# Shorter warm-up, earlier norms and reordered weight work in a one-core adaLN block (linear attention, then a dense Mish layer)

## The chip, the cores and the metric

The kernel runs on one core of one Trainium2 chip. The core has five engines that run side by side and wait for each other through semaphores: PE (TensorE, matrix products; its weight loads are listed as PEld), DVE (VectorE), ACT (ScalarE), POOL (GpSimd) and SP (SyncE, which here only asks for transfers). The metric is the device time of one execution in microseconds (us). All numbers are of the kernel as it was before the change.

## The reference

x has 2048 rows of 512 columns. A vector c gives six modulation rows. The first half is linear attention with 32 heads of 16 columns, the second a dense layer with Mish (512 to 1792 to 512):

```python
mod = (_silu(c) @ w_mod).reshape(c.shape[0], 6, 1, -1)
sa, ca, ga, sb, cb, gb = (mod[:, 0], mod[:, 1], mod[:, 2], mod[:, 3], mod[:, 4], mod[:, 5])
h = _layernorm(x, axis=-1) * (1 + ca) + sa
x = x + ga * _A_ref(h, A_wqkv, A_wo)
h = _layernorm(x, axis=-1) * (1 + cb) + sb
x = x + gb * _B_ref(h, B_w1, B_b1, B_w2)

# _A_ref, per head: phi(t) = where(t > 0, t + 1, exp(t)) + 1e-6
kv = phi(k)^T v;  z = sum of phi(k);  o = phi(q) kv / (phi(q) z + 1e-6);  out = o @ wo
# _B_ref
hid = x @ w1 + b1;  act = hid * tanh(softplus(hid));  out = act @ w2
```

## The kernel before

The 2048 rows are four blocks b of 512, and each block is four tiles t of 128 rows. A product in full precision is made of three in the fast 32-bit format: every operand is split into a high part (name ending in h, a cast on ACT or POOL) and a low part (ending in l, a subtraction on DVE), and PE adds high by high, high by low and low by high. So nearly every operand of PE passes through ACT or POOL and then DVE, and DVE has most of the work that isn't PE's.

The order on each engine is the order in which the program is written; nothing is rescheduled. Work that lies beside the main products is written as generators. `spawn` adds one to the running list, `spawn_idle` to a second list, and `tick` advances every running generator by one step and then the first two (later three) of the second list. So in one tick all that was spawned stands ahead of all that was spawned idle. All 128x512 tiles in SBUF come from one ring of 101 places (`SLOTS`); a load waits until the place it was given is free.

*Prologue (lines 111 to 620).* SP asks for x, the modulation weights and the first quarter of wqkv. Until the first data are there PE multiplies a tile of ones (`warm_up`, line 137): seven products, then the broadcast of silu(c) (`sc_bc`, line 148), then six (line 149). Block 0 is normalised tile by tile (`stats`, `act_sums`, `apply`), transposed on PE (`transposes_of`, line 498, with further warm-up products after the first two tiles), scaled by the modulation columns (`upper`, line 528, which needs mc from `mod_col`, line 179), and multiplied by wk into kp (lines 559 to 582). The first products of block 0 with x (`g_unit`, line 301, into gacc) need xn (the split of x) and pk (the split of phi(k)). `step(...)` advances single generators: `xsplit[t]` gives xn of tile t (its first step is the cast on POOL, its second the subtraction on DVE), `kpost[t]` gives phi(k) (ACT, then DVE's ku, then the cast pk_h on POOL and pk_l on DVE). Between these stands the normalisation of block 1: tiles 0 and 1 by `stats` on DVE, tiles 2 and 3 by `act_sums` on ACT; then `sums_eps` (DVE), the root on POOL (rs_x, line 205), `ln_shift` or `sums_shift` (DVE, nb_x), and `apply` on ACT. PE then transposes block 1 (line 243), and POOL and DVE split the result (hT), after POOL has made some constants (`make_constants`, line 158).

*First half of the dense layer (line 1197 on).* w1 and w2 are cut in seven pairs g of two times 128 hidden columns f. Each pair of hidden columns is computed for blocks 0 and 1 together with a seven-product scheme (`pair_unit`: p_a, p_s and the sums cb and c on DVE). PSUM has four tiles "acc", three "h" and one "tp", so a new p_s waits until DVE has read an older one (cb). The second product of block 0 (`d_unit`, into oacc) trails behind, by `trail`. For each f, `w2_job` (line 671) loads the 128 rows of w2, waits two ticks, multiplies them by gb on DVE (line 677), splits them and stores the halves to HBM. The first two are loaded ahead. SP's queue has, per pair, also the loads of w1 (w1p, `rows`), and the stores of w1's split parts (rd_, `store_rows`).

*Second product of block 1 (`second`, line 1182).* For f in the order 10 to 13, 0 to 9, PE multiplies a (block 1's hidden columns, split by `prep_a`) by w2, which is loaded back from HBM (w2b). Beside it `prepare` (line 1200) transposes the normalised blocks 2 and 3, `columns(2, c)` (line 954) makes the seven-product operands of these blocks from them (names b_2 and t_2, on ACT and DVE), and `w2_sums` makes sums of w2's rows. These operands are for the last part, blocks 2 and 3 together.

Of the kernel before, what the change touches and what calls it, by code (L numbers as in the profile page):

```python
# [18 lines left out]
NF = F // P  # L19
# [6 lines left out]
def block_kernel(ctx: ExitStack, tc: tile.TileContext, x, wqkv, wo, w1, b1t, w2, c, wmodt, out):  # L26
    nc = tc.nc
    act, dve, pool, pe, sp = nc.scalar, nc.vector, nc.gpsimd, nc.tensor, nc.sync
# [9 lines left out]
    def sb(name, dt=F32, shape=(P, 512)):  # L38

        return big.tile(list(shape), dt, tag="T", name=name, bufs=SLOTS)  # L40
# [9 lines left out]
    def spawn(gen):  # L50
        fresh.append(iter(gen))

    def spawn_idle(gen):

        idle_work.append(gen)
# [22 lines left out]
    def split(name, t, keep, key, lo_engine=dve, hi_engine=act, plus=None):  # L78

        hi, lo = sb(f"{name}h", F32R, t.shape), sb(f"{name}l", F32R, t.shape)  # L80
        if hi_engine is act:
            act.activation(hi, t, AF.Copy)
        else:
            hi_engine.tensor_copy(hi, t)
        if lo_engine is dve:
            yield
        if plus is None:
            lo_engine.tensor_tensor(lo, t, f32(hi), op=ALU.subtract)
        else:
            dve.scalar_tensor_tensor(lo, t, plus, f32(hi), op0=ALU.add, op1=ALU.subtract)  # L90
        keep[key] = hi, lo
# [45 lines left out]
    def warm_up(n):  # L137
        for i in range(n):
            pe.matmul(warm[:, P * (i % 4):P * (i % 4 + 1)], ones, ones, start=True, stop=True)
# [6 lines left out]
    dve.scalar_tensor_tensor(c2[0:1, :], th, 1.0, c0, op0=ALU.add, op1=ALU.mult)  # L146
    sc_bc = ps("acc", "sc_bc")
    pe.matmul(sc_bc, halves, c2, start=True, stop=True)
    warm_up(6)
    ident = cst.tile([P, P], F32, name="ident")  # L150
    make_identity(nc, ident)
    w32 = cst.tile([P, P], F32R, name="w32")
# [49 lines left out]
    def ln_rstd(key, b, lo=0, hi=4):  # L202

        y = rs[key, b][:, lo:hi]
        pool.tensor_tensor(y, y, half[:, lo:hi], op=ALU.pow)  # L205

    def ln_shift(key, b, lo=0, hi=4):

        dve.scalar_tensor_tensor(nb[key, b][:, lo:hi], mv[key, b][:, lo:hi, 0], -1.0, rs[key, b][:, lo:hi],  # L209
                                 op0=ALU.mult, op1=ALU.mult)  # L210

    def ln_apply(key, b, j, t, dst, engine):
        if engine is act:
            act.activation(dst, t, AF.Identity, bias=nb[key, b][:, j:j + 1], scale=rs[key, b][:, j:j + 1])  # L214
        else:
            engine.tensor_scalar(dst, t, mv[key, b][:, j, 0:1], rs[key, b][:, j:j + 1],
                                 op0=ALU.subtract, op1=ALU.mult)

    def act_sums(key, b, t, v):

        if (key, b) not in rs:
            for d, name in (rs, "rs"), (nb, "nb"):
                d[key, b] = cst.tile([P, 4], F32, tag=name, name=f"{name}_{key}_{b}", bufs=NB)
        scrap = sb(f"scrap_{key}_{b}_{t}")
        sums = cst.tile([P, 2], F32, tag="sums", name=f"sums_{key}_{b}_{t}", bufs=6)
        act.activation(scrap, v, AF.Identity, scale=-1.0 / D, accum_out=sums[:, 0:1])
        act.activation(scrap, v, AF.Square, bias=sums[:, 0:1], accum_out=sums[:, 1:2])
        return sums

    def sums_eps(key, b, t, sums):  # L230
        dve.tensor_scalar(rs[key, b][:, t:t + 1], sums[:, 1:2], 1.0 / D, EPS, op0=ALU.mult, op1=ALU.add)
        ln_rstd(key, b, t, t + 1)

    def sums_shift(key, b, t, sums):
        dve.tensor_tensor(nb[key, b][:, t:t + 1], sums[:, 0:1], rs[key, b][:, t:t + 1], op=ALU.mult)
# [31 lines left out]
    def k_post(p, b, t, hi_engine=act):  # L267
        u = ku[b, t] = sb(f"ku_{b}_{t}")
        yield from phi(p, f"k_{b}_{t}", u)
        yield from split(f"pk_{b}_{t}", u, pk, (b, t), hi_engine=hi_engine, plus=TINY)  # L270
        if b == NB - 1:
            dve.tensor_tensor(ku[0, t], ku[0, t], ku.pop((b, t)), op=ALU.add)
        elif b:
            pool.dma_start(ku[0, t], ku.pop((b, t)), accum_op=ALU.add)  # L274
# [189 lines left out]
    def stats(b, t):  # L464
        ln_stats("x", b, t, xt["x", b, t])
        ln_eps("x", b, t, t + 1)
        ln_rstd("x", b, t, t + 1)

    def apply(b, t, engine, shift=True):
        v = xt["x", b, t]  # L470
        if engine is act and shift:
            ln_shift("x", b, t, t + 1)
        ln_apply("x", b, t, v, v, engine)
# [24 lines left out]
    def transposes_of(*tiles):  # L498
        for t in tiles:
            for k in range(3):  # L500
                p = tp_late if k == 0 and t > 1 else tp0[k]
                pe.transpose(p[:, P * t:P * (t + 1)], xt["x", 0, t][:, P * k:P * (k + 1)], ident)
            warm_up(3 if t < 2 else 0)

    def mod_scale(k):
        mod_col(4 + k, sc_bc)
# [10 lines left out]
    xsplit = [split(f"xn_0_{t}", xt["x", 0, t], xn, (0, t), hi_engine=pool if t else act) for t in range(4)]  # L517

    def step(*gens):
        for g in gens:  # L520
            next(g, None)
# [49 lines left out]
    kpost = [k_post(kp[t], 0, t, pool) if t else k_post_first(kp[0]) for t in range(4)]  # L571
# [12 lines left out]
    step(xsplit[1], kpost[0], kpost[1])  # L584
    act.activation(sc_row, sc_bc, AF.Copy)
    stats(1, 0)
    step(kpost[0])
    sums2 = act_sums("x", 1, 2, xt["x", 1, 2])
    step(kpost[1], kpost[2])
    stats(1, 1)  # L590
    step(xsplit[1], kpost[1], kpost[3], xsplit[2])
    g_unit(0, 0)
    step(kpost[2])
    sums3 = act_sums("x", 1, 3, xt["x", 1, 3])
    sums_eps("x", 1, 2, sums2)
    ln_shift("x", 1, 0, 2)
    apply(1, 0, act, shift=False)
    apply(1, 1, act, shift=False)
    step(xsplit[2], kpost[2], xsplit[3])
    g_unit(0, 1)  # L600
    sums_eps("x", 1, 3, sums3)
    sums_shift("x", 1, 2, sums2)
    apply(1, 2, act, shift=False)
    step(kpost[3])
    sums_shift("x", 1, 3, sums3)
    apply(1, 3, act, shift=False)
# [60 lines left out]
    def load_w2(f):  # L667
        w2r[f] = sb(f"w2r_{f}")
        sp.dma_start(w2r[f], w2[P * f:P * (f + 1), :])

    def w2_job(f, wait=2):
        if f not in w2r:
            load_w2(f)
            for _ in range(wait):
                yield
        t = w2r[f]
        dve.tensor_tensor(t, t, bc["gb"], op=ALU.mult)
        yield
        yield from split(f"w2_{f}", t, w2s, f)
        yield  # L680
        g, n = f // 2, f % 2
        if n == 0:
            w2f[g] = drp.tile([P, 2, D], F32, name=f"w2f_{g}")
            for i in range(2):
                w2d[g, i] = drp.tile([P, 2, D], F32R, name=f"w2d_{g}_{i}")
        for i in range(2):
            pool.dma_start(w2d[g, i][:, n, :], w2s[f][i])
        if g < KEPT:
            pool.dma_start(w2f[g][:, n, :], t)
# [43 lines left out]
    def w2_again(f):  # L733

        w2s[f] = [sb(f"w2b_{f}_{i}", F32R) for i in range(2)]
        for i in range(2):
            pool.dma_start(w2s[f][i], w2d[f // 2, i][:, f % 2, :])  # L737
# [216 lines left out]
    def columns(c0, c, done):  # L954

        b11, b12, b21, b22 = [hf.pop((b, c + h)) for h in (0, 2) for b in (c0, c0 + 1)]
        t = [sb(f"t_{c0}_{c}_{i}") for i in range(4)]
        for d, u, v in (t[0], b12, b11), (t[1], b22, t[0]), (t[2], b22, b12), (t[3], b21, t[1]):
            dve.tensor_tensor(d, u, v, op=ALU.subtract)
        yield  # L960
        names = [("b11", b11), ("b21", b21), ("t1", t[0]), ("t2", t[1]), ("t3", t[2]), ("t4", t[3]), ("b22", b22)]
        halves = [split(f"{name}_{c0}_{c}", v, op_b, (name, c)) for name, v in names if name not in done]
        for n in range(0, len(halves) + 2, 2):
            for h in halves[max(n - 2, 0):n] + halves[n:n + 2]:
                next(h, None)
            yield
# [223 lines left out]
    def ahead(b, u):  # L1190

        if 0 <= u - NF + 4 < NF and last_first[u - NF + 4] < 2 * KEPT:
            w2_again(last_first[u - NF + 4])
        if 0 <= u - NF + 3 < NF:
            spawn(prep_a(b, last_first[u - NF + 3]))
# [4 lines left out]
    def prepare(f):  # L1200

        if f in (1, 3, 5, 7):
            for _ in range(2):
                transpose_f(*order.pop(0), "h")
        if f in (4, 8):
            spawn(columns(2, f // 4 - 1, ()))
        if f in W2_AT:
            spawn(w2_sums(W2_AT[f]))
        if f == NF - 2:
            load_rows(0)  # L1210
            load_wb(5)
        if f == NF - 1:
            load_wb(6)
# [15 lines left out]
    def trail(f, side=None, norm=True):  # L1229
        def unit():  # L1230
            if side is not None:
                if norm:
                    norm_next()
                spawn(side)
            d_unit(0, f, f)
            ahead(1, f)
        return unit

    for g in range(1, G):
# [217 lines left out]
```

## Time and profile before

| what | us |
|---|---|
| median of three runs | 494.65 |
| the three runs | 495.23, 494.62, 494.65 |
| the profiled execution, its own time | 495.11 |
| its span (first to last instruction) | 493.4 |
| DVE busy | 369.8 |
| ACT busy | 296.2 |
| POOL busy | 144.8 |

The span is what the trace shows; the execution's own time has some 1.7 us more around it. The granted clock of PE is 1.00 in every stretch of the trace. In a row of a timeline stand the start, the time, the engine, the line, the operation with the tiles that it writes and reads (buffer numbers left out, tile numbers kept where they follow an underscore), sizes, a count where equal rows follow each other, and in brackets how long the engine sat idle before it and what ended that. In a row of busy time by stretch stand the stretch, its length, the busy time of PE, PEld, DVE, ACT and POOL with the number of instructions, the granted clock, the share of the DMA engines' time and GB/s.

### The profile page before, as it was taken

The page shows a single profiled execution, that of the slowest core. Times are in us where ns is not written, and L with a number is a line of the kernel's source. Part 1 is how long each engine was busy: PE and PEld are TensorE (multiplying, and loading weights), DVE is VectorE, ACT ScalarE, POOL GpSimd, SP SyncE. Part 2 cuts the span into 40 slices and gives each one's busy share as a digit, 9 for nine tenths or more (in the row PEclk, how much of TensorE's full clock was granted, in tenths as well). Part 3 has the DMA queues.
Part 4 walks back from the last instruction along what each step waited for, and adds up shares of the span by engine and source line. Part 5 has one row for each costly group of instructions (what it writes and reads, how often), then busy time and mean ns, then how long its engine had stood idle before and what let it go on. Part 6 is the DMA issues. An engine that isn't in the chain of part 4 may idle for free.

```text
span 493.4 us, 7741 instructions
## 1 busy us (share of the span) xinstructions
PE 488.1 (99%) x2652; PEld 413.0 (84%) x2652; DVE 369.8 (75%) x717; ACT 296.2 (60%) x530; POOL 144.8 (29%) x244
## 2 busy tenths in 40 slices
PE   8999999999999999999999999999999999999997
PEld 7878888878878888888888878888888888899997
DVE  6888888999799698976877563789732666769872
ACT  6777587866546979738767655288045555568100
POOL 4493120000023123103432335214644410545200
PEclk9999999999999999999999999999999999999999
DMA  8714544144873417388899969999997704688512
GB/s 311 287 43 107 150 121 93 48 141 152 291 174 108 132 39 245 127 282 296 284 325 303 303 217 312 325 299 358 383 302 193 219 23 123 178 207 233 130 44 86
DMA packets 66785, 98.58 MB, mean 200 GB/s; under 512 B 7057, under 2 KB 31641, under 8 KB 66746
## 3 DMA queue, kind: packets, MB, share of 16 engines
q1 hardware_dynamic: 37896, 53.63, 32.9%
q0 software_dynamic: 28704, 44.19, 32.5%
q8 instruction: 21, 0.34, 0.3%
q10 hardware_dynamic: 146, 0.26, 0.1%
q14 instruction: 18, 0.15, 0.1%
HBM read 62.92 MB, written 33.03 MB: 194 GB/s over the span
## 4 chain that ended last, share of the span: by engine, by line
PE 97%; DVE 2%; POOL 1%; ACT 0%; issue 0%; ACTq 0%; POOLq 0%
PE p_a L1092 19%; PE p_s L1092 8%; PE oacc L76 5%; PE oacc L75 5%; PE oacc L74 5%; PE m L76 5%; PE m L75 5%; PE m L74 5%; PE o L74 3%; PE o L76 3%; PE o L75 3%; PE pq_a L371 3%; PE gacc L74 2%; PE gacc L76 2%; PE gacc L75 2%; PE pk L74 2%
## 5 line engine op out<-in xcount | busy, mean ns | idle before, releaser
L205 POOL TENSOR_TENSOR rs_n<-rs_n,half 128x1 f32<-128x1 f32 x16 | 11.4, 710 | 64.5 <-DVE rs_n L200 37.6
L1097 DVE TENSOR_TENSOR cb<-p_s,u 128x512 f32<-128x512 f32 x28 | 19.2, 686 | 12.8 <-ACT u L1133 12.8
L1127 ACT ACTIVATE u<-p_a 128x512 f32<-128x512 f32 x12 | 7.2, 598 | 28.3 <-PE p_a L1092 28.3
L1102 ACT ACTIVATE u<-p_a 128x512 f32<-128x512 f32 x14 | 8.4, 598 | 25.3 <-PE p_a L1092 25.3
L1084 ACT ACTIVATE ub<-cb,b1c 128x512 f32<-128x512 f32 x28 | 20.0, 718 | 5.8 <-DVE cb L1097 5.6
L1355 POOL DMA_DIRECT2D wt_m<-w2t x20 | 14.0, 702 | 26.8 <-DVE cb L1097 14.7
L949 ACT ACTIVATE hf_n<-tp_n,mc 128x512 f32<-128x512 f32 x16 | 11.7, 768 | 12.8 <-PE tp_n L947 12.8
L1133 ACT ACTIVATE u<-p_a 128x512 f32<-128x512 f32 x14 | 8.4, 596 | 17.0 <-PE p_a L1092 16.0
L737 POOL DMA_DIRECT2D w2b<-w2d x20 | 10.6, 534 | 24.0 <-PE tp_n L947 5.0
L1097 DVE TENSOR_TENSOR c<-p_a,u 128x512 f32<-128x512 f32 x14 | 9.6, 688 | 7.6 <-PE p_a L1092 6.5
L265 DVE SCALAR_TENSOR_TENSOR ku<-e_k,relu_k 128x512 f32<-128x512 f32 x15 | 10.7, 715 | 5.6 <-ACT relu_k L263 5.4
L849 POOL DMA_DIRECT2D rden_d<-rden x2 | 1.4, 718 | 45.7 <-DVE rden L847 45.7
L731 POOL DMA_DIRECT2D wb<-w2d x14 | 9.9, 710 | 14.7 <-PE p_a L1092 12.4
L1061 ACT ACTIVATE u<-p_a,b1c 128x512 f32<-128x512 f32 x14 | 9.6, 686 | 6.6 <-PE p_a L1092 6.6
L262 ACT ACTIVATE e_k<-pk 128x512 f32<-128x512 f32 x15 | 8.8, 589 | 7.8 <-PE pk L76 7.8
L214 ACT ACTIVATE x<-x,nb_x,rs_x 128x512 f32<-128x512 f32 x13 | 10.1, 810 | 5.4 <-DVE nb_x L209 3.8
L205 POOL TENSOR_TENSOR rs_x<-rs_x,half 128x1 f32<-128x1 f32 (+1 forms) x10 | 7.3, 736 | 20.4 <-DVE rs_x L200 19.6
L265 DVE SCALAR_TENSOR_TENSOR q<-e_q,relu_q 128x512 f32<-128x512 f32 x16 | 10.7, 684 | 3.1 <-ACT relu_q L263 3.1
L274 POOL DMA_DIRECT2D ku<-ku x8 | 7.2, 899 | 18.4 <-DVE ku L265 18.4
L873 DVE TENSOR_TENSOR r<-o,r 128x512 f32<-128x512 f32 x16 | 10.8, 676 | 1.0 <-PE o L76 0.9
L861 DVE SCALAR_TENSOR_TENSOR q<-q,rd 128x512 f32<-128x512 f32 x16 | 10.4, 683 | 1.4 <-DMA rd<-rden_d 1.4
L784 POOL DMA_DIRECT2D a1b<-rd_a x10 | 5.4, 539 | 19.0 <-PE p_a L1092 8.4
(1620 smaller groups left out, 1973.3 us busy)
## 6 DMA issues: line engine op xcount, KB each, us to landing
wm<-in_wmodt_dram SPq DMA_DIRECT2D x24, 256.0 KB, 5.2
w2b<-w2d POOLq DMA_DIRECT2D x20, 256.0 KB, 6.2
wt_m<-w2t POOLq DMA_DIRECT2D x20, 256.0 KB, 4.2
r<-in_x_dram SPq DMA_DIRECT2D x16, 256.0 KB, 2.9
x<-in_x_dram SPq DMA_DIRECT2D x15, 256.0 KB, 4.8
w1p<-in_w_dram SPq DMA_DIRECT2D x14, 256.0 KB, 3.5
w2r<-in_w_dram SPq DMA_DIRECT2D x14, 256.0 KB, 7.2
wb<-w2d POOLq DMA_DIRECT2D x14, 256.0 KB, 5.0
```

Source lines behind the costliest of these rows:

```text
L74: pe.matmul(o, st[0], mv[0], start=start, stop=False)
L75: pe.matmul(o, st[0], mv[1], start=False, stop=False)
L76: pe.matmul(o, st[1], mv[0], start=False, stop=stop)
L205: pool.tensor_tensor(y, y, half[:, lo:hi], op=ALU.pow)
L265: dve.scalar_tensor_tensor(dst, e, 1.0, r, op0=ALU.min, op1=ALU.add)
L371: pe.matmul(p, l, r, start=onto is None and c == 0 and i == 0, stop=c == 1 and i == 2, skip_group_check=onto is not None)
L873: dve.tensor_tensor(r, p, r, op=ALU.add)
L949: act.activation(hf[b, j], p, AF.Identity, bias=mc[:, 12 + j:13 + j], scale=mc[:, 16 + j:17 + j])
L1084: act.activation(u, p, AF.Mish, bias=b1c[:, f:f + 1])
L1092: pe.matmul(p, st, mv, start=onto is None and c == 0 and i == 0, stop=c == 1 and i == 2, skip_group_check=onto is not None)
L1097: dve.tensor_tensor(out, p, u, op=ALU.add)
L1355: pool.dma_start(v, w2t[g][:, :, SUM[name], :])
```

## The change

There are four edits.

1. `warm_up` after sc_bc makes four products instead of six; after the transposes of tiles 0 and 1 it makes two and one instead of three and three.
2. In the first block's tail, the steps are reordered. On POOL the cast xn_2h stands ahead of pk_1h instead of behind it, and the root for block 1's tile 3 stands ahead of xn_3h instead of behind it. On DVE `sums_eps` of tile 2 stands ahead of xn_1l instead of behind ku of tile 2, `sums_shift` of tile 2 directly behind `ln_shift`, and `sums_eps` of tile 3 ahead of pk_2l. Block 1's tiles 0, 1 and 2 are normalised on ACT in one go, behind the sums of tile 3 as before.
3. `load_w2` for f = 10 and 11 is called behind `d_unit` of f = 6, that of 12 and 13 behind f = 8. `w2_job` finds them loaded, and still waits its two ticks. On SP's queue the loads of 10 and 11 now stand directly behind those of 8 and 9, ahead of the loads of w1's last pair and the eight stores of pair 4; those of 12 and 13 stand behind these stores.
4. `columns(2, c)` is spawned idle. On DVE and ACT each a_4 to a_9 stands ahead of the operands of the last blocks that it stood behind, by up to two operations.

No operation is added on any engine; five products on PE are gone.

```diff
-    warm_up(6)
+    warm_up(4)
...
-            warm_up(3 if t < 2 else 0)
+            warm_up((2, 1, 0, 0)[t])
...
     stats(1, 0)
-    step(kpost[0])
+    step(xsplit[2], kpost[0])
     sums2 = act_sums("x", 1, 2, xt["x", 1, 2])
     step(kpost[1], kpost[2])
     stats(1, 1)
-    step(xsplit[1], kpost[1], kpost[3], xsplit[2])
+    sums_eps("x", 1, 2, sums2)
+    step(xsplit[1], kpost[1], kpost[3])
     g_unit(0, 0)
     step(kpost[2])
+    ln_shift("x", 1, 0, 2)
+    sums_shift("x", 1, 2, sums2)
     sums3 = act_sums("x", 1, 3, xt["x", 1, 3])
-    sums_eps("x", 1, 2, sums2)
-    ln_shift("x", 1, 0, 2)
-    apply(1, 0, act, shift=False)
-    apply(1, 1, act, shift=False)
-    step(xsplit[2], kpost[2], xsplit[3])
+    for t in range(3):
+        apply(1, t, act, shift=False)
+    step(xsplit[2])
+    sums_eps("x", 1, 3, sums3)
+    step(kpost[2], xsplit[3])
     g_unit(0, 1)
-    sums_eps("x", 1, 3, sums3)
-    sums_shift("x", 1, 2, sums2)
-    apply(1, 2, act, shift=False)
     step(kpost[3])
...
     def w2_job(f, wait=2):
         if f not in w2r:
             load_w2(f)
+        if f > 1:
             for _ in range(wait):
                 yield
...
         if f in (4, 8):
-            spawn(columns(2, f // 4 - 1, ()))
+            spawn_idle(columns(2, f // 4 - 1, ()))
...
             d_unit(0, f, f)
             ahead(1, f)
+            if f > 5 and f % 2 == 0:
+                for i in (4, 5):
+                    if f + i < NF:
+                        load_w2(f + i)
```

## The prediction

> **What bounds the kernel now.** I read the page first, then the waits of PE (TensorE), then the timelines of PE and its feeders where PE stood still.
>
> ```profile
> span 493.4 us, 7741 instructions
> PE 488.1 (99%) x2652; PEld 413.0 (84%) x2652; DVE 369.8 (75%) x717; ACT 296.2 (60%) x530; POOL 144.8 (29%) x244
> ...
> PE tp_x L243 <- ACT x L214: 0.4, 1, 0.4
> PE gacc L308 <- POOL pk_2h L84: 0.3, 1, 0.3
> PE p_s L1092 <- DVE cb L1097: 0.2, 1, 0.2
> ```
>
> PE is busy 99% of the span, and after its first instruction it has three waits of 0.2 to 0.4 us. Only two things can therefore bring time: fewer PE instructions on the path, or those few holes. A matmul's printed time overlaps with the next one's, so a hole's cost is read from starts: 128x512 products that follow each other start 0.227 us apart (four from 26.96 would end their turn at 27.87 in the rows below).
>
> **1. Fewer warm-up products.**
>
> ```profile
> 1.09 3.36 PE L139 MATMUL warm<-ones 128*128 128x128 f32 x14 [1.09 <-POOL ones L131]
> ...
> 6.37 1.76 PE L139 MATMUL warm<-ones 128*128 128x128 f32 x12
> 8.30 0.83 PE L139 MATMUL warm<-ones 128*128 128x128 f32 x6
> 10.28 0.30 PE L502 MATMUL tp_late<-ident,x 128*128 128x128 f32 x1
> 10.88 0.70 PE L563 MATMUL pk<-wk_0h,hT_x_0h 128*128 128x512 f32 x2
> ...
> 6.67 2.65 ACT L214 ACTIVATE x<-x,nb_x,rs_x 128x512 f32<-128x512 f32 x3
> 10.95 0.56 ACT L530 ACTIVATE hT_x_0h<-tp_late,mc 128x256 fp32r<-128x256 f32 x1 [1.10 <-PE tp_late L502]
> 12.30 0.79 ACT L530 ACTIVATE hT_x_1h<-tp_x,mc 128x512 fp32r<-128x512 f32 x1
> ...
> 10.78 0.68 DVE L181 SCALAR_TENSOR_TENSOR wm<-wm,sc_bc 128x512 f32<-128x512 f32 x1
> ```
>
> After sc_bc the calls of warm_up ask for 6+3+3 products, and now for 4+2+1: five fewer, ten instructions in the trace, where each product is two (6 show as x12). Six take from 8.30 to about 8.97, 0.112 us each, so at most 1.12 us goes. The path has a floor: the transposes of tile 2 need ACT's third normalisation, which ends at 6.67+2.65 = 9.32. PE would be there at 10.28-1.12 = 9.16, waits, and starts tp_late at about 9.37 where it started at 10.28: 0.91 earlier. ACT sat idle 1.10 us for just this transpose, so it follows. The next floor is hT_x_1h: its modulation column comes from DVE at 10.78+0.68 = 11.46, and no part of the change moves that, so ACT's 12.30 can become 11.5 and not less. I take 0.80 us, with bounds 0 (a later floor I overlook) and 1.12. What is late next is DVE's chain of columns and low halves, which also follows ACT's rows; the loads it reads were asked for earlier and do not move.
>
> **2. Second block's norms earlier.**
>
> ```profile
> 26.96 1.07 PE L308 MATMUL gacc<-pk_1l,xn_1h 128*128 128x512 f32 x4
> 28.36 1.19 PE L308 MATMUL gacc<-pk_2h,xn_2h 128*128 128x512 f32 x4 [0.33 <-POOL pk_2h L84]
> 31.21 0.49 PE L243 MATMUL tp_x<-ident,x 128*128 128x128 f32 x3
> 32.06 1.64 PE L243 MATMUL tp_x<-ident,x 128*128 128x128 f32 x13 [0.36 <-ACT x L214]
> 34.47 1.08 PE L308 MATMUL gacc<-pk_3h,xn_3l 128*128 128x512 f32 x4
> ...
> 23.93 0.61 POOL L84 CAST pk_1h<-ku 128x512 fp32r<-128x512 f32 x1 [3.23 <-DVE ku L265]
> 25.84 0.70 POOL L84 CAST xn_2h<-x 128x512 fp32r<-128x512 f32 x1
> 27.16 1.14 POOL L84 CAST pk_2h<-ku 128x512 fp32r<-128x512 f32 x1 [0.61 <-DVE rs_x L231]
> 29.46 1.06 POOL L205 TENSOR_TENSOR rs_x<-rs_x,half 128x1 f32<-128x1 f32 x1
> 33.77 0.61 POOL L84 CAST hT_x_0h<-hf_x 128x512 fp32r<-128x512 f32 x1
> ...
> 25.99 1.10 DVE L265 SCALAR_TENSOR_TENSOR ku<-e_k,relu_k 128x512 f32<-128x512 f32 x1
> 27.02 0.14 DVE L231 TENSOR_SCALAR rs_x<-sums_x 128x1 f32<-128x1 f32 x1
> 31.19 0.81 ACT L214 ACTIVATE x<-x,nb_x,rs_x 128x512 f32<-128x512 f32 x1 [0.83 <-DVE nb_x L235]
> ```
>
> The first hole: PE was due at 27.87 and began at 28.36, and those four took 0.12 more than the four before; 0.61 us in all. It waited for POOL's pk_2h, which waited for DVE's ku. That ku took 1.10 us where the DVE operation of that kind at 10.78 took 0.68, and xn_2h ran on POOL beside it. xn_2h now goes ahead of pk_1h, into POOL's 3.23 us of idleness, so ku should lose some 0.4 us. Against it stand one more tiny DVE operation ahead of ku (sums_eps, 0.14 at 27.02) and a second rs_x on POOL behind pk_1h (up to 1.06, the row at 29.46), which takes the place of xn_2h (0.70) and so still ends about when ku does. I take 0.35 us, bounds -0.14 and 0.61.
>
> The Trainium skill, page SBUF — State Buffer, section "SBUF: two separate sides", says that DVE and GpSimd share a port pair as an exclusive lock, held for the whole instruction, and that the loser blocks. The rows agree for ku (1.10) and pk_2h (1.14 against 0.61 for pk_1h). By it pk_2h itself may stay slow, since DVE's xn_2l still follows ku; the sum would lose nothing that it counts.
>
> The second hole: three transposes at 0.11 us from 31.21 end their turn at 31.54, and the fourth came at 32.06, with 0.05 more to get going: 0.57 us. It waited for the normalised tile 3, which ACT began at 31.19 because rs_x stood at 29.46 on POOL behind pk_2h and xn_3h. In the new order rs_x comes directly behind pk_2h and tile 2's bias is long done, so ACT can start tile 3 once POOL and DVE have done one small operation each: pk_2h's end, 28.30 less 0.35, plus 1.06 and 0.14 is 29.15, two us earlier. I take all 0.57, bounds 0 and 0.57. Late next is POOL's hT_x_0h at 33.77, behind pk_3h and the constants; pk_3h leaves that same rs_x behind it, so this row moves up by about 1 us, more than PE gains here.
>
> **3. w2's last rows.**
>
> ```profile
> 257.49 1.05 SPq L669 DMA_DIRECT2D w2r<-in_w_dram  x2
> 258.71 8.82 SPq L744 DMA_DIRECT2D w1p<-in_w_dram  x2
> 273.48 10.09 SPq L669 DMA_DIRECT2D w2r<-in_w_dram  x4
> DMA to landing us min/median/max: 3.6/5.8/7.8
> ...
> 281.07 0.69 DVE L677 TENSOR_TENSOR w2r<-w2r,gb_bc 128x512 f32<-128x512 f32 x1 [1.18 <-DMA w2r<-in_w_dram]
> 283.00 0.69 DVE L677 TENSOR_TENSOR w2r<-w2r,gb_bc 128x512 f32<-128x512 f32 x1 [1.24 <-DMA w2r<-in_w_dram]
> 289.11 0.68 DVE L1097 TENSOR_TENSOR cb<-p_s,u 128x512 f32<-128x512 f32 x1
> ...
> 289.26 0.39 PE L1092 MATMUL p_a<-b_3h,a_6l 128*128 128x512 f32 x1
> 289.85 0.50 PE L1092 MATMUL p_s<-t_0h,s_6h 128*128 128x512 f32 x1 [0.19 <-DVE cb L1097]
> ```
>
> DVE lost 1.18+1.24 = 2.42 us to w2's rows 10 and 11, then worked without a pause, and its cb ended 0.36 us too late (289.85-289.26-0.23), with 0.11 for the restart: 0.47 us. The loads of 10 and 11 now stand on SP behind those of 257.49, ahead of the two w1p and the eight stores; those of 12 and 13 behind the stores. One of the two waits for a ring place, as w1p did; even if both left as late as the second w1p (267.5) and took 7.8 us, they land at 275.3, before DVE wants them (279.9). Behind them on SP wait w1p of pair 6, which then leave by about 268, as before. The same bytes move, so I charge DMA with nothing. I take 0.47; bounds 0 and 0.47.
>
> **4. Last blocks' operands behind all else.**
>
> ```profile
> 346.61 0.68 DVE L88 TENSOR_TENSOR a_8l<-ub,a_8h 128x512 fp32r<-128x512 f32 x1
> 346.96 0.39 PE L75 MATMUL oacc<-w2b,a_8h 128*128 128x512 f32 x1
> 347.35 0.50 PE L76 MATMUL oacc<-w2b,a_8l 128*128 128x512 f32 x1
> 340.00:352.00 12.00, 12.00 (x53) 9.45 (x52) 11.96 (x20) 5.30 (x10) 8.26 (x15) 1.00 1.20 367
> ```
>
> DVE is full here (11.96 of 12 us), and a_8l came 0.16 us late, plus 0.11: 0.27 us. In the new order two operations that start 0.60 us apart no longer stand before a_8l, so it comes 1.2 us earlier. No instruction is added. The operands put behind are for products after 352 and all done in the same ticks. I take 0.27, bounds 0 and 0.27.
>
> **Sum.** 0.80+0.35+0.57+0.47+0.27 = 2.46 us. The profiled execution took 495.11 us, 1.7 more than its span, so it becomes 492.65. The median of before is 494.65, from 495.23, 494.62 and 494.65: two groups half a us apart. If that half is noise everywhere, the sum gives 492.2; if it lies in the first 10 us, where PE's early pace decides and the change leaves ACT as the floor, 492.65. I say 492.5.
>
> **The rivals.** (a) The prologue's gain stops short: part 1 gives 0 because a load or DVE becomes the floor. For it: DVE is the tight engine there. Against: ACT's 1.10 us of waiting was for PE. Time 492.5+0.8 = 493.3. (b) The two late parts bring nothing (0.74): the transfers are late in the new place too, or another DVE operation is as late. Against: 4.6 us of margin at 275.3. Time 493.2. (c) DVE cannot follow in the second block: PE arrives 2.2 us earlier (all but part 4), DVE's full stretch does not move, and a_8l (1.2 earlier) leaves PE standing 2.2-1.2+0.1 = 1.1 us. Time 492.5+0.27+1.1 = 493.9. Against: the stretch begins behind ACT's copies of PE's transposes, so it moves with PE. (d) The other side: PE loses its pace. In the first 3.4 us an instruction takes 0.24 us, later 0.112: PE starts at half pace. The warm-ups fill the time between transposes; with fewer of them PE is idle for some 0.4 us more, in short pieces, between 8.3 and 9.4. If PE falls to half pace near 10 us for a stretch of 7 us, it loses 3.5 us, and the time is 496.0. It decides for slower from a stretch of (495.64-492.5)x2 = 6.3 us on; the start, from 1.09 to 6.37 at least, shows that 5.3 are possible. Against: from 31.21 to 33.45 PE had only transposes and a hole of 0.52, and four products then took 1.08 us, as before.
>
> On (d), the Trainium skill's page TensorE: Matmul & The Clock Gate, section "Part 4: PE-mode transpose", says that transposes do not count as PE-busy in the same way, and its Part 1 that PE drops to half clock after an idle window of about 3.4 us. By that rule (d) is likelier than a count of instructions suggests; the row at 34.47 speaks against it, since the clock held there. (e) The change does not do what it says: each engine's order is moved as the words have it, but each hole reappears one step later, and only the 0.35 of xn_2h is kept: 494.3. Against: two of the four holes have DVE rows without a pause behind them, so a shift of DVE passes through.
>
> **How the numbers follow.** All main terms land: 0.62, and 492.5, with a range of its own of 491.9 to 493.2. (a) 0.12, (b) 0.09, (c) 0.05, (d) 0.06, (e) 0.06. What a measurement can tell from no change is about 0.2%, 1.0 us, so faster means under 493.66. Main, (a) and (b) lie there: 0.83, less 0.01 for their upper ends. (c) and (e) are within: 0.11, with 0.01 from (a). Slower is (d) and a rest: 0.07. The range goes from 491.6 (all upper bounds, 1.12+0.61+0.57+0.47+0.27 = 3.04, off 494.65) to 493.9.
>
> **What would show it.** Right: tp_late near 9.4, hT_x_1h near 11.5, the two holes near 28 and 31 gone or under 0.3 us, no DVE wait for w2r and PE's p_s directly behind p_a near 287, no hole at a_8l. Wrong: PE instructions of the first matmuls at twice their pitch (d), or a new wait of PE on DVE near 345 (c) or on POOL's hT rows near 34 (e).

## The result, and the profile after

| | before | changed |
|---|---|---|
| median of seven runs, us | 494.68 | 493.52 |
| lowest to highest | 494.52 to 495.59 | 493.07 to 494.08 |
| ratio, 95% interval | | 0.997 (0.9958 to 0.9981) |
| span of the profiled execution | 493.4 | 492.0 |

By the medians the change makes the kernel 1.2 us faster. The forecast was 492.5, in a range of 491.6 to 493.9.

PE does the same products in the same order in both kernels, but for five warm-up products. So the gain can be followed by one product at a time: its start before, its start after.

| PE's product | before | changed | earlier by |
|---|---|---|---|
| tp_late, first transpose of tile 2 | 10.28 | 9.38 | 0.90 |
| pk by hT_x_1h | 13.23 | 12.49 | 0.74 |
| pk by hT_x_1l | 16.08 | 15.47 | 0.61 |
| first gacc (pk_0h, xn_0h) | 22.42 | 22.38 | 0.04 |
| gacc by pk_2h | 28.36 | 28.24 | 0.12 |
| gacc by pk_3h and xn_3l | 34.47 | 33.78 | 0.69 |
| p_a by a_6l, last before the stop at 289 | 289.26 | 288.67 | 0.59 |
| p_s by s_6h, first behind it | 289.85 | 288.89 | 0.96 |
| oacc by a_8l | 347.35 | 346.01 | 1.34 |

The 0.90 us of the warm-ups were there at 10 us and were gone at 22. Of the second part the tile 3 half stayed (0.12 to 0.69), and the two late parts stayed too. The page and PE's waits of the changed kernel:

```profile
span 492.0 us, 7721 instructions
...
PE 487.3 (99%) x2642; PEld 411.7 (84%) x2642; DVE 370.8 (75%) x717; ACT 296.4 (60%) x530; POOL 146.1 (30%) x244
...
PE gacc L308 <- POOL pk_2h L84: 0.2, 1, 0.2
```

Of PE's three waits, those for tile 3's norm and for cb are gone; that for pk_2h is left.

**Where the first 0.9 us went.** The timelines of the changed kernel, PE's first, then DVE's low halves and POOL's work on wk:

```profile
12.49 1.17 PE L563 MATMUL pk<-wk_1h,hT_x_1h 128*128 128x512 f32 x4
14.42 1.08 PE L570 MATMUL pk<-wk_0h,hT_x_0l 128*128 128x512 f32 x4
15.47 1.20 PE L570 MATMUL pk<-wk_1h,hT_x_1l 128*128 128x512 f32 x4
...
19.48 0.74 PE L575 MATMUL pk<-wk_3h,hT_x_3l 128*128 128x512 f32 x2
...
22.38 1.12 PE L308 MATMUL gacc<-pk_0h,xn_0h 128*128 128x512 f32 x4
...
11.59 1.44 DVE L551 TENSOR_TENSOR hT_x_0l<-hf_x,hT_x_0h 128x512 fp32r<-128x512 f32 x1
14.34 1.08 DVE L551 TENSOR_TENSOR hT_x_1l<-hf_x,hT_x_1h 128x512 fp32r<-128x512 f32 x1
17.73 1.09 DVE L88 TENSOR_TENSOR xn_0l<-x,xn_0h 128x512 fp32r<-128x512 f32 x1
18.75 0.68 DVE L551 TENSOR_TENSOR hT_x_3l<-hf_x,hT_x_3h 128x512 fp32r<-128x512 f32 x1
...
10.48 0.62 POOL L84 CAST wk_1h<-wr 128x512 fp32r<-128x512 f32 x1 [1.42 <-DMA wr<-in_wqkv_dram]
11.18 1.30 POOL L88 TENSOR_TENSOR wk_1l<-wr,wk_1h 128x512 fp32r<-128x512 f32 x1
```

The same of the kernel before:

```profile
12.45 0.69 DVE L551 TENSOR_TENSOR hT_x_0l<-hf_x,hT_x_0h 128x512 fp32r<-128x512 f32 x1 [0.98 <-ACT hf_x L530]
...
14.46 0.94 DVE L551 TENSOR_TENSOR hT_x_1l<-hf_x,hT_x_1h 128x512 fp32r<-128x512 f32 x1
...
9.96 0.61 POOL L84 CAST wk_1h<-wr 128x512 fp32r<-128x512 f32 x1 [0.92 <-DMA wr<-in_wqkv_dram]
10.66 1.29 POOL L88 TENSOR_TENSOR wk_1l<-wr,wk_1h 128x512 fp32r<-128x512 f32 x1
```

DVE used to sit idle for 0.98 us before hT_x_0l. ACT now has its operand ready 0.86 us sooner, and DVE begins at 11.59 where it began at 12.45. But there it meets POOL's wk_1l, which runs to 12.48, and takes 1.44 us where it took 0.69. hT_x_1l starts 0.12 earlier than before, takes 1.08 for 0.94 beside POOL's wk_2l, and ends at 15.42, 0.02 later than before (15.40). Before, PE asked for it at 16.08; now PE is there at 15.34 (the four of 14.42 and 4 times 0.23), waits, and starts at 15.47. xn_0l (1.09 us) stands before hT_x_3l, which ends at 19.43, and PE, due at 19.35, starts at 19.48. Each stop also costs some 0.1 for the restart: the second product behind it comes 0.34 us after the first, where 0.23 is the rule. POOL, for its part, was 0.52 us later than before, because the load of wk_1 landed later. No part of the change touches that load, and the changed kernel's second profile (below) has the cast at 10.05.

**The second block.** ku has its normal length, pk_2h has not, and tile 3 is in time. The changed kernel's rows of POOL, DVE, ACT and PE, and then one of DVE in the kernel before:

```profile
21.02 0.61 POOL L84 CAST xn_2h<-x 128x512 fp32r<-128x512 f32 x1
27.04 1.15 POOL L84 CAST pk_2h<-ku 128x512 fp32r<-128x512 f32 x1 [0.26 <-DVE nb_x L209]
...
21.14 1.03 DVE L285 SCALAR_TENSOR_TENSOR pk_0h<-e_k,relu_k 128x512 fp32r<-128x512 f32 x1 [0.71 <-ACT relu_k L282]
26.29 0.68 DVE L265 SCALAR_TENSOR_TENSOR ku<-e_k,relu_k 128x512 f32<-128x512 f32 x1
...
27.04 0.68 DVE L88 TENSOR_TENSOR xn_2l<-x,xn_2h 128x512 fp32r<-128x512 f32 x1
...
30.10 0.82 ACT L214 ACTIVATE x<-x,nb_x,rs_x 128x512 f32<-128x512 f32 x1 [0.55 <-DVE nb_x L235]
...
28.24 1.20 PE L308 MATMUL gacc<-pk_2h,xn_2h 128*128 128x512 f32 x4 [0.19 <-POOL pk_2h L84]
...
31.10 1.91 PE L243 MATMUL tp_x<-ident,x 128*128 128x128 f32 x16
```

```profile
21.25 0.69 DVE L285 SCALAR_TENSOR_TENSOR pk_0h<-e_k,relu_k 128x512 fp32r<-128x512 f32 x1 [1.18 <-ACT relu_k L282]
```

In its new place POOL's xn_2h no longer runs beside ku, but it runs beside DVE's pk_0h, which starts 0.11 us earlier than before and takes 1.03 for 0.69. This, and sums_eps (0.07), which now stands before xn_1l, puts DVE's row back, and ku starts at 26.29 for 25.99. The four experiments below show that it is this part of the change that does it: pk_0h takes 1.04 in the one with the norms moved and 0.69 in the other three.

The 16 transposes run as one group from 31.10; before, they were three, a stop, and thirteen.

**The two late parts.** SP's, DVE's and PE's rows of the changed kernel:

```profile
256.80 6.20 SPq L669 DMA_DIRECT2D w2r<-in_w_dram  x4
...
279.22 1.29 DVE L678 TENSOR_TENSOR w2r<-w2r,gb_bc 128x512 f32<-128x512 f32 x2
...
288.67 0.39 PE L1093 MATMUL p_a<-b_3h,a_6l 128*128 128x512 f32 x1
288.89 0.39 PE L1093 MATMUL p_s<-t_0h,s_6h 128*128 128x512 f32 x1
...
344.45 0.68 DVE L88 TENSOR_TENSOR a_8l<-ub,a_8h 128x512 fp32r<-128x512 f32 x1
...
345.79 0.39 PE L75 MATMUL oacc<-w2b,a_8h 128*128 128x512 f32 x1
346.01 0.39 PE L76 MATMUL oacc<-w2b,a_8l 128*128 128x512 f32 x1
```

The loads of w2's rows 10 and 11 leave with those of 8 and 9, DVE takes both rows one behind the other with no wait, and PE's p_s follows p_a by 0.22 us. a_8l ends at 345.13, 0.9 us before PE wants it.

### The profile page after: what moved, and what is told of

Read it like the earlier page. It is cut to its first block, busy times and chain, and to the rows that moved or that the text cites. A ratio compares the mean times of both kernels' runs of the same rounds, so it can differ in the third digit from the quotient of the medians.

```text
span 492.0 us, 7721 instructions
## 1 busy us (share of the span) xinstructions
PE 487.3 (99%) x2642; PEld 411.7 (84%) x2642; DVE 370.8 (75%) x717; ACT 296.4 (60%) x530; POOL 146.1 (30%) x244
## 4 chain that ended last, share of the span: by engine, by line
PE 96%; DVE 2%; ACT 1%; POOL 0%; ACTq 0%; issue 0%
PE p_a L1093 19%; PE p_s L1093 8%; PE oacc L75 5%; PE oacc L76 5%; PE oacc L74 5%; PE m L76 5%; PE m L75 5%; PE m L74 5%; PE o L74 3%; PE o L76 3%; PE o L75 3%; PE pq_a L371 3%; PE gacc L74 2%; PE gacc L76 2%; PE pk L76 2%; PE gacc L75 2%
```

## The experiments

Theory F says: in the prologue DVE's row of columns and low halves is the floor, and PE cannot keep what the warm-ups gave. Theory L adds: the floor moves with the landing of wk_1's load, because POOL's wk_1l follows the load and DVE's hT_x_0l is held up by wk_1l. Rival N is the term of the prediction, 0.80 us kept.

**Each part alone, in the kernel before.** The first:

```diff
-    warm_up(6)
+    warm_up(4)
...
-            warm_up(3 if t < 2 else 0)
+            warm_up((2, 1, 0, 0)[t])
```

> The kernel before with the fewer warm-up products alone. Theory F (floor): DVE's row of modulation columns and low halves up to hT_x_3l sets when PE may go on, whatever else happens; PE is some 0.8 us early at 12 us and has given nearly all of it back by its first gacc product, which starts between 22.3 and 22.4 us (22.42 before); time 494.6, no more than 0.15 below before. Rival L (landing): the profile of the changed kernel had wk_1's load land 0.5 us later by chance (POOL's cast at 10.48, before 9.96), and POOL's later row slowed DVE; where the cast starts near 9.96, the first gacc product comes at 22.0 or earlier and the time is 494.0 to 494.3. Rival N (the prediction's term): 0.80 us kept, first gacc at 21.6, time 493.9.

Measured: 494.42, ratio 0.9988 (0.9977 to 0.9999); the first gacc at 22.28 with the cast of wk_1h at 10.44. Of the 0.78 us that PE had at tp_late (9.50 for 10.28) 0.14 were left, so in this execution N is out. The time alone does not show it: the median is 0.62 below that of the kernel before beside it (495.04), and the interval allows 0.05 to 1.1.

The second has the whole reordering of steps from the change:

```diff
-    step(kpost[0])
+    step(xsplit[2], kpost[0])
...
+    sums_eps("x", 1, 2, sums2)
+    step(xsplit[1], kpost[1], kpost[3])
...
+    for t in range(3):
+        apply(1, t, act, shift=False)
```

> The kernel before with the norms moved alone. The second hole (tile 3's transposes) goes: 0.5 to 0.57 us. For the first hole (pk_2h at 28 us) theory F says: DVE's ku is no longer slowed (0.68 for 1.10), but pk_2h's cast on POOL still takes about 1.1 since DVE's xn_2l runs beside it; with DVE's row not pushed back by the prologue the hole shrinks from 0.49 by 0.3 to 0.4: together 0.85 to 0.95, time 493.7 to 493.9. Rival: the first hole stays at 0.36 or so as in the changed kernel, whatever the prologue did, since the added bias and norm operations of DVE take back what ku gains: together 0.63, time 494.0.

Measured: 494.75, ratio 0.9996 (0.9984 to 1.0008): nothing. The trace shows why. The second hole is gone and the first has shrunk only a little, so that the transposes behind them come 0.67 us earlier than in the kernel before, and 0.12 of it PE had already at the first gacc (22.30). The 0.55 between is the rival's side, and what took ku's gain is pk_0h beside xn_2h, as above. And then at 285 and 289 us most of the gain is lost again, by DVE's and PE's rows of this kernel:

```profile
282.22 1.32 DVE L677 TENSOR_TENSOR w2r<-w2r,gb_bc 128x512 f32<-128x512 f32 x2 [3.09 <-DMA w2r<-in_w_dram]
...
289.68 0.50 PE L1092 MATMUL p_s<-t_0h,s_6h 128*128 128x512 f32 x1 [0.45 <-DVE cb L1097]
```

PE came earlier, the load of w2's rows did not: DVE waited 3.09 us for it instead of 2.42, and p_s started only 0.17 us before its time in the kernel before. Without the third part the second is worth little in such an execution.

The third:

```diff
             load_w2(f)
+        if f > 1:
             for _ in range(wait):
                 yield
...
             ahead(1, f)
+            if f > 5 and f % 2 == 0:
+                for i in (4, 5):
+                    if f + i < NF:
+                        load_w2(f + i)
```

> The kernel before with w2's last rows asked for sooner alone. Theory: no DVE wait for w2r after 275 us, PE's p_s near 289 follows p_a by 0.23 us instead of 0.58, its restart of 0.11 goes too: 0.45 us, time 494.2. Rival: it is moved to a later hole in this kernel, whose blocks 8 and on are unchanged: under 0.15 us, time 494.6.

Measured: 494.60, ratio 0.9985 (0.9974 to 0.9996). DVE does not wait for w2's rows 10 and 11, and p_s at 289.70 has no stop before it. It did wait for rows 8 and 9, which no edit moves, 0.25 and 1.01 us:

```profile
267.09 0.69 DVE L678 TENSOR_TENSOR w2r<-w2r,gb_bc 128x512 f32<-128x512 f32 x1 [1.01 <-DMA w2r<-in_w_dram]
```

PE did not stop for it. The stop at 289 differs from one execution to the next where this part is missing: DVE's wait for rows 10 and 11 was 2.42 us in the profile before, 1.80 in the first experiment, 3.09 in the second and none in the fourth, and PE stopped only where it was 2.42 or more. In the ten profiles with this part there is neither. Of the four experiments' times these have the least spread, 0.8 us.

The fourth:

```diff
-            spawn(columns(2, f // 4 - 1, ()))
+            spawn_idle(columns(2, f // 4 - 1, ()))
```

> The kernel before with the columns of the last blocks' operands put behind all else alone. Theory: both short stops at 344 to 348 us go, 0.27 to 0.38 us, time 494.3 to 494.4. Rival: DVE is full there, and the operands put behind come late for PE after 350 us: a new stop of 0.3 or more, time 494.6 or above.

Measured: 495.04, ratio 0.9993 (0.9981 to 1.0006). In the trace the stop at a_8l is gone, a smaller one at a_7l too, and nothing new stands behind them. The times of these four cannot be told apart: each ranges over 0.8 to 2.0 us, and the runs of the kernel before beside them over 2.9 (494.11 to 496.98, median 495.04). The traces carry the argument, and one trace can mislead: this execution took 493.77, and its span of 492.0 is that of the changed kernel's profile, though it has only the fourth part. Its load of wk_1 was early (the cast at 10.08), and it had no stop at 289.

There is also a stop that neither the prediction nor any edit is about. At 195 us PE waits for DVE's qs_2l:

```profile
195.49 0.50 PE L76 MATMUL o<-m_2h,qs_2l 128*128 128x512 f32 x1
```

The same products from 190 to 200 us took 0.14 us longer in the profile of before than in the ten profiles without this stop, 0.16 in the changed kernel's, 0.28 in its second (below) and 0.39 in that of the third experiment.

**The old warm-ups in the changed kernel.**

```diff
-    warm_up(4)
+    warm_up(6)
...
-            warm_up((2, 1, 0, 0)[t])
+            warm_up(3 if t < 2 else 0)
```

> The changed kernel with the old number of warm-up products. Theory F (DVE's row is the floor of the prologue): the first gacc product starts where it does in the changed kernel, between 21.9 and 22.5 us by the landing of wk_1's load and not by the warm-ups; time as the changed kernel's within 0.2. Rival N (the fewer products are worth their 0.8): first gacc at 23.1 or later where PE's early pace is slow, time 0.6 to 0.8 above the changed kernel's.

Measured: 493.32, ratio 0.9968 (0.9958 to 0.9979), so as fast as the changed kernel. Its rows of POOL and PE:

```profile
10.08 0.61 POOL L84 CAST wk_1h<-wr 128x512 fp32r<-128x512 f32 x1 [1.03 <-DMA wr<-in_wqkv_dram]
...
22.23 1.09 PE L308 MATMUL gacc<-pk_0h,xn_0h 128*128 128x512 f32 x4
```

PE was 0.64 us later at tp_late (10.02) than in the changed kernel, and 0.15 us earlier at the first gacc. The time and the first gacc speak against N. But the cast stood at 10.08, and with the cast at 10.05 the changed kernel (next) has its first gacc 0.30 earlier; 0.18 of that is left at pk_2h. So F holds only in part: about half of the 0.65 at tp_late came through here.

**The changed kernel once more, unaltered.**

> The changed kernel once more, unaltered, beside the three below, so that they have its time on the same chip and its scatter is seen. Theory L+F (the landing of wk_1's load, which differs by half a us from one execution to the next, sets where POOL's work meets DVE's, and DVE's row sets PE): the first gacc product at 21.9 to 22.2 us if POOL's cast of wk_1h starts at 10.2 or earlier, at 22.2 to 22.4 if it starts at 10.4 or later; time 493.3 to 493.5. Rival: the first gacc does not follow the landing.

Measured: 493.36 (492.90 to 494.34), ratio 0.9955 (0.9939 to 0.9972). The kernel before, beside it, had a median of 495.86, so here the change is worth 2.5 us by the medians. POOL, DVE and PE:

```profile
10.05 0.62 POOL L84 CAST wk_1h<-wr 128x512 fp32r<-128x512 f32 x1 [1.00 <-DMA wr<-in_wqkv_dram]
10.75 1.30 POOL L88 TENSOR_TENSOR wk_1l<-wr,wk_1h 128x512 fp32r<-128x512 f32 x1
...
11.58 1.02 DVE L551 TENSOR_TENSOR hT_x_0l<-hf_x,hT_x_0h 128x512 fp32r<-128x512 f32 x1
...
21.93 1.13 PE L308 MATMUL gacc<-pk_0h,xn_0h 128*128 128x512 f32 x4
```

The same kernel, with the cast 0.43 us earlier, has its first gacc 0.45 us earlier. hT_x_0l began at the same time and ended at 12.60, 0.55 us behind the end of wk_1l (12.05); in the first profile it ended at 13.03, 0.55 behind 12.48. In the experiments with the norms alone and w2 alone it began later, at 12.09 and 12.14, and ended 0.54 behind wk_1l all the same. So DVE waits for the end of POOL's instruction, whenever it began beside it. All ten profiles that share the loads and the order up to the first gacc:

| kernel | warm-ups | tp_late | cast of wk_1h | first gacc | gacc less cast |
|---|---|---|---|---|---|
| changed, again | new | 9.37 | 10.05 | 21.93 | 11.88 |
| xn_2l later (below) | new | 9.37 | 10.18 | 22.05 | 11.87 |
| warm-ups alone | new | 9.50 | 10.44 | 22.28 | 11.84 |
| ku earlier (below) | new | 9.51 | 10.47 | 22.36 | 11.89 |
| changed | new | 9.38 | 10.48 | 22.38 | 11.90 |
| w2 alone | old | 9.96 | 10.51 | 22.36 | 11.85 |
| norms alone | old | 9.91 | 10.43 | 22.30 | 11.87 |
| columns alone | old | 9.82 | 10.08 | 21.99 | 11.91 |
| old warm-ups | old | 10.02 | 10.08 | 22.23 | 12.15 |
| before | old | 10.28 | 9.96 | 22.42 | 12.46 |

With the new warm-ups the first gacc is always 11.84 to 11.90 us behind the cast. With the old ones it is so too, unless PE is late and the load early. By this table the fewer products are worth the difference, up to 0.6 us in an execution like the profiled one of before (12.46 less 11.87), and nothing in three of the five with old warm-ups.

**xn_0l behind hT_x_3l.** From here the diffs are against the changed kernel.

```diff
-        if k == 2:
-            step(xsplit[0])
...
+    step(xsplit[0])
     kpost = [k_post(kp[t], 0, t, pool) if t else k_post_first(kp[0]) for t in range(4)]
```

> The changed kernel with xn_0l, which DVE makes at 17.73 us ahead of hT_x_3l, put behind it. Theory F: hT_x_3l ends 0.3 us or more earlier, PE's stop at 19.12 us (0.36 instead of 0.23, and 0.11 for the restart) goes, first gacc 0.25 us earlier for the same landing; time 0.25 lower. Rival L: what is late is DVE's hT_x_0l and hT_x_1l at 11.6 to 15.4, and the time given back later is only their echo: then nothing changes, under 0.1.

Measured: 493.13, ratio 0.9961 (0.9948 to 0.9975). DVE and PE:

```profile
18.07 0.69 DVE L551 TENSOR_TENSOR hT_x_3l<-hf_x,hT_x_3h 128x512 fp32r<-128x512 f32 x1 [0.58 <-ACT hf_x L530]
...
21.78 1.07 PE L308 MATMUL gacc<-pk_0h,xn_0h 128*128 128x512 f32 x4
```

The cast stood at 10.16, so the table's rule gives 22.03; it was 0.25 us earlier, as theory F had it. At pk_2h half of that was given back: the first gacc was 0.60 us earlier than in the changed kernel (0.35 of it by the earlier load), that by pk_2h (27.77 for 28.24) 0.47.

**xn_2l behind pk_2l.**

```diff
-    step(xsplit[2])
     sums_eps("x", 1, 3, sums3)
-    step(kpost[2], xsplit[3])
+    step(kpost[2], xsplit[2], xsplit[3])
```

> The changed kernel with DVE's xn_2l put behind pk_2l, so that nothing that reads two tiles of SBUF runs on DVE beside POOL's cast of pk_2h. Theory S (DVE and POOL hold each other up when they meet): the cast takes 0.61 instead of 1.15 us, PE's stop at 28.2 (0.36, and 0.11 behind it) goes; xn_2l then ends near 28.9, before PE's turn for it at 28.8 to 29.0; time 0.3 to 0.5 lower. Rival: the cast takes 1.1 whoever runs beside it (its operand is new), or xn_2l becomes the stop, 0.2 or more at 28.8; time the same within 0.15.

Measured: 493.34, ratio 0.9969 (0.9957 to 0.9981). POOL's and PE's rows:

```profile
26.74 0.61 POOL L84 CAST pk_2h<-ku 128x512 fp32r<-128x512 f32 x1 [0.26 <-DVE nb_x L209]
...
27.58 1.09 PE L308 MATMUL gacc<-pk_2h,xn_2h 128*128 128x512 f32 x4
28.74 1.20 PE L308 MATMUL gacc<-pk_2h,xn_2l 128*128 128x512 f32 x4
```

With xn_2l out of its way the cast takes 0.61 us, so it was the meeting that made it 1.15, and PE's stop at 28.2 is gone. But then xn_2l comes late: four products from 27.58 end their turn at 28.49, the next came at 28.74, with a restart behind it. Both sides were half right, and the time is the old one.

**wk_1's load one place earlier.**

```diff
     load_wmod(4 + k)
+    if k == 1:
+        load_wqkv(1, k)
     load_wmod(k)
-    load_wqkv(1, k)
+    if k != 1:
+        load_wqkv(1, k)
```

> The changed kernel with wk_1's load asked for one place earlier, ahead of a column's weights (wm_1). Theory L: POOL's cast of wk_1h starts 0.68 us earlier for the same start of the loads (9.3 to 9.8 us), POOL's wk_1l is through when DVE begins hT_x_0l, which takes 0.7 to 1.0 instead of 1.44; first gacc 0.3 to 0.45 earlier than in the changed kernel (near 21.95), time lower by that. Rival F: DVE's row meets POOL's somewhere else, hT_x_1l stays near 15.4 and the first gacc at 22.3 to 22.4; time the same within 0.15. Rival W: wm_1 is now late, DVE waits for it near 10.8, first gacc later than 22.4.

Measured: 493.01 (492.92 to 493.08), ratio 0.9960 (0.9945 to 0.9975), the lowest of its set. DVE and POOL:

```profile
9.39 1.10 DVE L88 TENSOR_TENSOR wk_0l<-wr,wk_0h 128x512 fp32r<-128x512 f32 x1
...
11.80 0.69 DVE L554 TENSOR_TENSOR hT_x_0l<-hf_x,hT_x_0h 128x512 fp32r<-128x512 f32 x1
...
9.34 0.61 POOL L84 CAST wk_1h<-wr 128x512 fp32r<-128x512 f32 x1 [0.28 <-DMA wr<-in_wqkv_dram]
```

hT_x_0l is free of POOL (0.69), as L had it. But the cast now begins 0.05 us ahead of DVE's wk_0l, and that takes 1.10: the meeting has moved. The first gacc is at 22.09, between L's 21.95 and F's 22.3.

**ku of tile 2 ahead of pk_1l; two and three edits together.**

```diff
-    step(xsplit[1], kpost[1], kpost[3])
+    step(xsplit[1], kpost[2], kpost[1], kpost[3])
     g_unit(0, 0)
-    step(kpost[2])
```

> The changed kernel with DVE's ku of tile 2 ahead of pk_1l (0.60 us earlier), which POOL's pk_2h waits for. Theory: the cast of pk_2h starts near 26.4 instead of 27.04 and is done by 27.6 even at 1.15 us, ahead of PE's turn at 27.89; the stop there (0.36 and 0.11) goes and pk_1l is just in time; PE's transposes at 31 come 0.45 earlier and tile 3's norm still meets them; time 0.45 lower. Rival: pk_1l comes late by as much (a stop of 0.1 to 0.3 at 27), or the 0.45 is given back at the transposes at 31 us; time lower by 0.2 or less.

Measured: 493.10, ratio 0.9949 (0.9931 to 0.9967), beside 493.36 for the changed kernel on the same chip. The stop at pk_2h is gone; pk_1l costs a stop of 0.1 and its restart at 27. Of the expected 0.45 some 0.3 came.

> The changed kernel with wk_1's load a place earlier and xn_0l behind hT_x_3l. Theory F: the part of the fewer warm-ups that DVE took back comes free: first gacc at 21.6 to 21.8 (22.38), but the stop at pk_2h grows to 0.5, since DVE's row behind the first ku follows ACT and not the low halves; time 0.4 to 0.6 lower than the changed kernel's. Rival: one alone brings all there is, the same as v4_load (first gacc 22.09, 0.5 lower).

Measured: 493.20, ratio 0.9951 (0.9932 to 0.9969). The expected first gacc was missed: 22.05. POOL's cast started at 9.24 and DVE's wk_0l took 1.10 again; the column for hT_x_1h was late by that, and PE stood at 12.9. The rival is right: together they bring no more than the load alone did (493.01, in another set of runs).

> The three edits together (v6_ku2 and v7_two). Theory: they add up, 0.8 to 1.1 us below the changed kernel, 492.4 to 492.7, and no stop of PE over 0.3 us between 10 and 36 us. Rival: PE then waits for the next thing, tile 3's norm at 31 us or the low halves hT of block 1 at 35 to 37, 0.3 to 0.5 us; 493.0.

Measured: 492.63, ratio 0.9943 (0.9923 to 0.9963); five of the six runs lie from 492.47 to 492.86, below the lowest of the changed kernel beside it (492.90), the sixth at 493.96. The page, POOL, DVE and PE:

```profile
span 490.8 us, 7719 instructions
...
9.45 1.10 POOL L84 CAST wk_1h<-wr 128x512 fp32r<-128x512 f32 x1 [0.40 <-DMA wr<-in_wqkv_dram]
...
9.39 0.68 DVE L88 TENSOR_TENSOR wk_0l<-wr,wk_0h 128x512 fp32r<-128x512 f32 x1
...
21.65 1.07 PE L311 MATMUL gacc<-pk_0h,xn_0h 128*128 128x512 f32 x4
...
27.47 1.08 PE L311 MATMUL gacc<-pk_2h,xn_2h 128*128 128x512 f32 x4
```

This is the fastest version, by 0.7 us below the changed kernel's median in its set, a little under the 0.8 to 1.1 expected; the first gacc is 0.28 us earlier than in the second profile of the changed kernel, that by pk_2h 0.36 (27.83 there). The two spans differ by 0.9, and 0.28 of this is the stop at 195 us, which this execution did not have; whether an edit or chance took it away is not shown. Here the load landed a little later than in the two kernels above, the cast began at 9.45, behind wk_0l, and it was the cast that took 1.10 and DVE that lost nothing. How much of the 0.7 depends on that was not tried.

## Why the prediction was right, and where it was not

The direction was right, and the time lies in the range, but near its upper end and outside the range of 491.9 to 493.2 that the prediction gave for the case where all main terms land. That case did not come: two of the five terms were almost wholly lost, and what came is near rival (a). So the mechanism was right for three terms, and that the number fell within the range is owed in part to the width given for the rivals.

*Fewer warm-ups, 0.80 us forecast: 0.04 by the first gacc.* The steps up to hT_x_1h were right: tp_late at 9.38 (9.37 forecast), hT_x_1h's product 0.74 us earlier (0.80). What failed is the sentence on what is late next: DVE's chain "also follows ACT's rows; the loads it reads were asked for earlier and do not move". DVE did follow ACT, by 0.86 us, but ran into POOL's wk_1l and lost 0.75 of it. And the load of wk_1 does move between executions: by the cast, by 0.43 us between the two profiles of the changed kernel. Rival (a), a load or DVE as the floor, is what came, and its time of 493.3 is near the 493.52 measured. It was given a chance of 0.12: the prediction named DVE as the tight engine there, but took ACT's idle time as proof that PE was the limit, and did not look for the next engine at PE's new time. The execution it was read from was also the one with most to gain: tp_late stood at 10.28 there, and at 9.82 to 10.02 in the other four profiles with the old warm-ups.

*ku, 0.35 forecast: 0.1.* ku lost its 0.42, as said, and took 0.68. But it began 0.30 later (26.29 for 25.99), and the cast behind it still met xn_2l. That the cast might stay at 1.15 was in the prediction. What failed is the step that put xn_2h "into POOL's 3.23 us of idleness" at no cost: POOL was idle there, but DVE was not, and pk_0h lost 0.34 us to the cast. The prediction charged DVE with sums_eps alone.

*Tile 3's norm, 0.57: 0.57* (0.12 to 0.69 in the table of products). Forecast as the bound and reached; ACT began the tile at 30.10, not at 29.15, which was early enough.

*w2's last rows, 0.47.* From 0.59 to 0.96, and the restart of 0.11 behind it: 0.48. The term was right for the profiled execution; in the four profiles without this part the stop was there in two (0.47 and, with the norms moved, 0.71 with its restart) and absent in two, and it came in none of the ten with it. So the part also keeps the second part's gain alive.

*Columns, 0.27.* From a_8h, 346.96 to 345.79, to a_8l, 0.17, and the restart: 0.28, as forecast. The stop at a_7l, which the sum had not counted, was another 0.1.

The terms came to 2.46; 1.4 us of the span went. The difference is nearly all of the first term and most of ku's; the 0.1 of a_7l made up for 0.1 that PE lost in small pieces between 34 and 289 us. Rivals (c) and (d) did not come: a_8l is early, and behind 10 us no group of four products took the double of its 1.07 us. (b) is out by the rows of the late parts, and (e) for three of the holes: those at 31, 289 and 347 us have not come back at another place. At the one at 28 us something like (e) came: the gain of xn_2h, the one that (e) let stand, was mostly given back.

## What to carry to other kernels

A gain ahead of a full engine is kept only as far as that engine's own row lets it: carry the earlier start through each engine in turn, and check with which other work every instruction now runs side by side. An engine's idle time is a free place only if the other engine is idle there too, where the two hold each other up. One profile is one landing of its loads; where PE, DVE and a transfer arrive within half a us of each other, the next execution has another one of them last, so edits should be judged by several profiles. A stop that depends on a transfer can swallow a gain made 250 us earlier, so take away the late waits first.

## What the runs showed of the hardware

DVE's operations on two tiles in SBUF and POOL's casts and subtractions did not slow each other by a share: the second waited for the first. hT_x_0l ended 0.55 us behind POOL's wk_1l in both profiles of the changed kernel (12.60 and 12.05, 13.03 and 12.48), pk_0h 0.54 behind xn_2h (22.17 and 21.63), and wk_0l at 9.39 lost 0.42 us to a cast that began at 9.34, while a cast that began at 9.45 lost 0.49 to wk_0l. DVE's weighted sums with sc_bc, which lies in PSUM, took 0.68 beside the same POOL work. The Trainium skill, page SBUF — State Buffer, section "SBUF: two separate sides", states just this: whichever of a DVE operation with two SBUF inputs and a GpSimd operation starts first holds the shared port pair for its whole length. So here a cast that began 0.11 us later changed which engine paid.

PE's early pace changes at another time in each execution. Its first product began at 1.09 us or within 0.01 of it in all profiles. The eight instructions of the second warm-up took 1.26 us in the profile of the changed kernel and 1.05 in that of xn_0l moved, where they were at full pace from the first:

```profile
6.38 1.26 PE L139 MATMUL warm<-ones 128*128 128x128 f32 x8
...
5.47 1.05 PE L139 MATMUL warm<-ones 128*128 128x128 f32 x8
```

Over the 14 profiles the change of pace, from 0.21 to 0.11 us for a 128x128 product, lies between 4.2 and 7.0 us. Of the five profiles with the old warm-ups only that of before was held up by it: its first transposes started at 7.97, behind the warm-ups. In the other four they started at 7.42 to 7.66, some 0.05 behind ACT's first norm, and tp_late followed at 9.82 to 10.02. Under the new warm-ups tp_late lies between 9.37 and 9.51, with ACT's norms as the floor. The Trainium skill, page TensorE: Matmul & The Clock Gate, Part 1, has the clock rise at the end of a free-running window of about 3.4 us, so at another point of each run; the rows agree, and their spread of 2.8 us fits into one such window.
